# Squared products taken out of PSUM by one ScalarE operation, fp32 masked scores in the second batch, another bank for the last outputs

## The chip, the core and the metric

The program runs on one core of a Trainium2 chip. TensorE multiplies, VectorE and ScalarE do element-wise work, GpSimd clears small tiles, and SyncE issues the transfers. The engines run side by side, each taking its own instructions in order and waiting on semaphores for the others. The metric is the time of one execution in microseconds (us), as the median of several.

## The reference

Three layers follow one another for each of four batches of 768 rows and 384 columns (8 heads of 48):

```python
# 1. a recurrence over the rows t, per batch and head, with a 48x48 complex state
S_re, S_im = ar * S_re - ai * S_im + k[t] v[t]^T, ar * S_im + ai * S_re
y[t] = q[t] @ S_re
# 2. mixing of rows, then of channels
u  = x + (relu(x^T @ w_tok1) @ w_tok2)^T
z  = u + relu(u @ w_ch1) @ w_ch2
# 3. a gated layer on z mixed with the row before it
xk, xr = mu_k * z + (1 - mu_k) * z_prev, mu_r * z + (1 - mu_r) * z_prev
out = sigmoid(xr @ w_r) * (relu(xk @ w_k) ** 2 @ w_v)
```

## The kernel before

**The attention** turns the recurrence into products. The rows of a batch are cut into six blocks of 128 (J = 0 to 5). Sums of the logarithms of the decays (tiles X1, X2, X3) give factors for q and k. For each block, VectorE and ScalarE make q and k in two fp16 parts, a high and a low one (`qh`, `ql`, `kh`, `kl`); the DMA engines transpose them into the tile Rc; TensorE makes the scores `sp` of four heads at a time (stage `s_f`, groups g = 0 and 1); VectorE masks them into `m` (`s_m`, L656); and TensorE multiplies them with v into the output bank `y` (`s_h`, L668), to which the product of q with the carried state is added. `s_u` and `s_v` carry the state on, in the bank `u`. `s_i` (L689) takes `y` out of PSUM as `xh` and `xl`.

In batch 0 the masked scores meet v in fp32: one product a head. In batches 1 to 3 they are split into two fp16 parts in Rc: a ScalarE copy in `s_m` and a VectorE subtraction in `s_g` (L662). Then three fp16 products a head are made, high with high, high with low and low with high, with v split in the same way (`vh`, `vl`, `s_w`). The bank of `sp`, the bank of `y` and the place of the split scores exist once in these batches.

**The dense layers** run after the attention of their batch, beside the attention of the next one. In `two_layers` (L803) a first product makes a hidden tile of 128 columns and 384 rows in one of two PSUM banks (`ps`); it is taken out of PSUM as two fp16 parts (`part`, shown as `g`); and two tiles later the second product uses these. For w_k the way out is `wk1_out` (L907): ScalarE rectifies `ps` in place, squares it in place and copies it to the high part, then VectorE subtracts to get the low part. Only then is the bank free for the next but one hidden tile.

**What sets the order.** `ORD0` and `ORD1` list the stages of an attention step with the block each works on (`h01` is `s_h` with g = 0 on the block before). Each generator yields estimated costs, and the dense layers and the attention are interleaved by these. A scheduler places the instructions on the engines by priorities (`P_PE`, `P_EV`). So instructions near an edit can change places on every engine. The loads of the next batch's decays (`X<-by_time_a_re`) are issued behind the transposes of blocks 3 and 5. ScalarE squares them when they have landed, and VectorE adds the squares (`X3<-X3,wide`) and takes a minimum (`stat_rmin`).

Batches are counted from 0 in the code (`b`); "the second batch" below is b = 1.

Of the kernel before, what the change touches and what calls it, by code (L numbers as in the profile page):

```python
# [8 lines left out]
F32 = mybir.dt.float32  # L9
# [9 lines left out]
C = H * D  # L19
# [81 lines left out]
def split_path(  # L101
# [38 lines left out]
    tri32 = [const.tile([128, 128], F32, name=f"tri32{i}") for i in range(2)]  # L140
    ones32 = [const.tile([128, 128], F32, name=f"ones32{i}") for i in range(2)]
    last32 = const.tile([128, 128], F32, name="last32")
    anti = const.tile([128, 128], F16, name="anti")
# [56 lines left out]
    def setup_small():  # L200
        nc.sync.dma_start(out=col_c, in_=c_col)
        t = tmps.tile([128, 512], F32, tag="tmp", name="tri32")
        nc.sync.dma_start(out=t[:, 0:384], in_=c_tri)
        nc.gpsimd.tensor_copy(tri, t[:, 0:128])
        nc.gpsimd.tensor_copy(anti, t[:, 128:256])
        for i, sc in enumerate((2.0 ** L_S, 2.0 ** F_S / (2.0 * math.pi))):
            ACT(tri32[i], t[:, 0:128], ACTF.Copy, scale=sc)
            nc.gpsimd.memset(ones32[i], sc)
        ACT(last32, t[:, 256:384], ACTF.Copy)
        for t in qk16.values():  # L210
            nc.gpsimd.memset(t, 0.0)
# [116 lines left out]
    def attention(b):  # L328
# [201 lines left out]
        def load(J, names):  # L530
            if J < NJ:
                d = st.setdefault(J, {})
                ts = slice(128 * J, 128 * J + 128)
                if "q" in names:
                    t = two.tile([128, 2, C], F32, tag="hl", name="qk") if b == 0 else CH[:, 0:2]
                    d["q"], d["k"] = hd(t[:, 0]), hd(t[:, 1])
                    queue(nc.sync.dma_start(out=t, in_=qk[b, ts]))
                if "v" in names:
                    t = CH[:, J % 2 if b == 0 else 2]
                    d["v"] = hd(t)  # L540
                    queue(nc.sync.dma_start(out=t, in_=v[b, ts]))
# [24 lines left out]
        def s_b(J):  # L566
            d = st[J]
            d["vh"], d["vl"] = hd(v16[:, J % 2]), hd(v16[:, 2 + J % 2])
            d["q2"], d["k2"] = (W[:, i].rearrange("p h c d -> p c h d") for i in range(2))
            if b > 0 or J == 0:  # L570
                turn(J)
            for nm, X, i in (("q", X3, 0), ("k", X1, 1)):
                w = hd(X[:, J])
                STT(w, d[nm], col_c[:, i:i + 1], w, op0=MUL, op1=MUL)
            if b > 0:
                load(J + 1, "q")
            return 1.33

        def s_w(J):
# [3 lines left out]
            if J == 0:  # L583
                seen(d["vh"][:, :, 0:LOW_N // H])
            if b > 0:
                load(J + 1, "v")
# [67 lines left out]

        def s_m(J, g):
            m = st[J]["m", g] = tmps.tile([128, 512], F32, tag="tmp", name="m").rearrange("p (i t) -> p i t", i=4)  # L656
            TT(m, st[J]["S", g], tri.unsqueeze(1).to_broadcast([128, 4, 128]), op=MUL)
            if b > 0:
                ACT(M16[g][0], m, ACTF.Copy)
            return 0.6  # L660

        def s_g(J, g):  # L662
            if b == 0:
                return 0.0
# [3 lines left out]
        def s_h(J, g):  # L668
            d = st[J]
            if g == 0:  # L670
                d["y"] = bank("y", J, [128, H, D])
            y = d["y"]
            with tc.high_priority(offset=P_PE):
                for h in range(4 * g, 4 * g + 4):
                    if J > 0:
                        th, tl = hd(T16[0:96, J % 2]), hd(T16[0:96, 2 + J % 2])
                        for n_, (a_, b_) in enumerate((("h", th), ("h", tl), ("l", th))):
                            MM(out=y[:, h], lhsT=Tr[J % 2]["q" + a_][0:96, h], rhs=b_[:, h], start=n_ == 0, stop=False)
                    if b == 0:
                        MM(out=y[:, h], lhsT=d["m", g][:, h % 4], rhs=d["v32"][:, h], start=J == 0, stop=True)  # L680
                    for n_, (m_, v_) in enumerate(((0, "vh"), (0, "vl"), (1, "vh")) if b > 0 else ()):
                        MM(out=y[:, h], lhsT=M16[g][m_][:, h % 4], rhs=d[v_][:, h], start=J == 0 and n_ == 0, stop=n_ == 2)
            return 0.0

        def s_i(J):
            d = st.pop(J)
            if J == 0:
                x_hl[b] = [one.tile([128, NJ, C], F16, tag=f"x{s}", name=f"x{s}") for s in "hl"]
# [21 lines left out]
        fns.update({nm + str(g): late(fn, g) for nm, fn in (("f", s_f), ("g", s_g), ("h", s_h), ("m", s_m)) for g in range(2)})  # L710
        order = [(x[0], fns[x[:-1]], int(x[-1])) for x in (ORD0 if b == 0 else ORD1).split()]

# [16 lines left out]
        load(0, "qv")  # L729
        if b == 0:  # L730
            load(1, "qv")
        if b == 0:
# [18 lines left out]
    def dense(b):  # L751
# [44 lines left out]
        def two_layers(nf, first, second, evac1, evac2, at=None):  # L796
# [3 lines left out]
            for n_ in range(len(items) + LAG):  # L800
                if n_ < len(items):
# [4 lines left out]
                    with tc.high_priority(offset=P_EV):  # L806
                        evac1(ps, part)
                        if n_ == 0:
# [25 lines left out]

        def ch1_out(ps, part):
            ACT(part[:, 0], ps, ACTF.Relu)  # L836
# [69 lines left out]

        def wk1_out(ps, part):  # L907
            ACT(ps, ps, ACTF.Relu)  # L908
            ACT(ps, ps, ACTF.Square, scale=2.0 ** (SQ_S // 2 - XK_S - WK_S))
            ACT(part[:, 0], ps, ACTF.Copy)  # L910
            last_ev[:] = [TT(part[:, 1], ps, part[:, 0], op=SUB)]  # L911

# [333 lines left out]
```

## Time and profile before

| | |
|---|---|
| time, median of 3 runs | 816.45 us (816.13 to 817.19) |
| profiled execution: its own time, and the span of its trace | 818.82 us, 817.0 us |
| TensorE busy | 741.3 us (91%) |
| VectorE busy | 581.8 us (71%) |
| ScalarE busy | 522.6 us (64%) |
| mean granted TensorE clock, of full speed | 0.974 |

Busy times count the engines' instructions; the ends of matrix products are modelled, and they overlap, so a busy TensorE may still be slower than its best. Up to about 125 us the first batch's attention runs almost alone; from there to about 320 us run the first batch's dense layers with the second batch's attention, and so on; the last batch's dense layers run alone. In the rows L337 and L482 are helpers through which the attention's instructions pass, so these are told apart by their tiles.

### The profile page before, as it was taken

How to read it: one execution, taken by the hardware profiler on the slowest of the kernel's cores; microseconds unless marked ns; L12 is line 12 of the kernel's file. 1: busy time of each engine (PE TensorE's matmuls, PEld its weight loads, DVE VectorE, ACT ScalarE, POOL GpSimd, SP SyncE). 2: the span in 40 equal slices, each digit the busy share in tenths (PEclk: the TensorE clock that was granted, in tenths of full speed). 3: DMA queues.
4: the chain of work that ended last, by engine and by line, in shares of the span. 5: the costliest groups of instructions: out<-in, count | busy, mean ns of one | idle time of the engine just before them, and what ended most of it. 6: DMA issues, size and time to landing. Idle time of an engine off the chain costs nothing.

```text
span 817.0 us, 15178 instructions
## 1 busy us (share of the span) xinstructions
PE 741.3 (91%) x6107; PEld 471.4 (58%) x6107; DVE 581.8 (71%) x1016; ACT 522.6 (64%) x988; POOL 21.3 (3%) x53
## 2 busy tenths in 40 slices
PE   0968878999989889999998989999999999999996
PEld 0557845455555455555665656566666666666553
DVE  3998978999998738887768448777776454484822
ACT  7884559777588779674568778566576532142752
POOL 3000000001010000000000000000000000010000
PEclk9987989999999999999999989999999999999998
DMA  8249983444673851052336331141333342868200
GB/s 273 78 118 205 195 264 136 130 154 118 176 137 82 194 120 49 20 122 55 62 63 120 91 85 49 46 104 26 63 62 63 81 134 79 268 198 261 103 30 33
DMA packets 137949, 94.92 MB, mean 116 GB/s; under 512 B 104592, under 2 KB 120208, under 8 KB 137872
## 3 DMA queue, kind: packets, MB, share of 16 engines
q1 hardware_dynamic: 137872, 93.88, 45.2%
q8 instruction: 50, 0.82, 0.4%
q14 instruction: 27, 0.22, 0.1%
HBM read 63.97 MB, written 4.72 MB: 84 GB/s over the span
## 4 chain that ended last, share of the span: by engine, by line
PE 47%; DVE 21%; ACT 15%; DMA 12%; issue 3%; SPq 1%; DVEq 0%; ACTq 0%
PE ps L741 22%; PE a L741 14%; PE y L482 4%; DVE X L337 4%; ACT X L337 3%; DMA X<-by_time_a_re_dram 3%; PE u L482 3%; DMA wst<-in_moe_w_k_dram 2%; DVE Wc L337 2%; PE sp L482 2%; ACT tmp L875 2%; DMA Rc<-qh 1%; DVE g L837 1%; DMA wst<-in_moe_w_v_dram 1%; DVE ql L337 1%
## 5 line engine op out<-in xcount | busy, mean ns | idle before, releaser
L741 PEld LDWEIGHTS <-wc 128*128 128x128 f16 x1728 | 166.7, 98 | 116.9 <-issue 9.5
L741 PE MATMUL ps<-uh,wc 128*128 128x384 f16 x576 | 156.3, 326 | 2.1 <-DVE ul L793 1.2
L741 PE MATMUL a<-g,wc 128*128 128x384 f16 x864 | 157.9, 326 | 0.0
L741 PE MATMUL ps<-xkh,wk 128*128 128x384 f16 x384 | 106.4, 331 | 3.5 <-DVE g L911 3.3
L741 PE MATMUL a<-wv,g 128*128 128x384 f16 x576 | 106.9, 328 | 2.5 <-ACT g L910 2.5
L836 ACT ACTIVATE g<-ps 128x384 f16<-128x384 f32 x96 | 46.4, 484 | 78.0 <-PE ps L741 76.6
L741 PE MATMUL ps<-ul,wc 128*128 128x384 f16 x288 | 93.8, 326 | 0.0
L482 PEld LDWEIGHTS <-Rc 96*128 96x128 f16 (+1 forms) x1416 | 69.8, 100 | 34.4 <-issue 13.9
L837 DVE SCALAR_TENSOR_TENSOR g<-ps,g 128x384 f16<-128x384 f32 x96 | 52.9, 554 | 37.4 <-ACT g L836 37.2
L741 PEld LDWEIGHTS <-wk 128*128 128x128 f16 x576 | 55.6, 99 | 39.9 <-issue 6.4
L741 PEld LDWEIGHTS <-g 128*128 128x128 f16 x576 | 54.9, 98 | 37.4 <-ACT g L910 3.0
L741 PE MATMUL ps<-xkl,wk 128*128 128x384 f16 x192 | 63.5, 331 | 0.0
L911 DVE TENSOR_TENSOR g<-ps,g 128x384 f16<-128x384 f32 x64 | 35.3, 553 | 35.1 <-ACT g L910 34.9
L482 PE MATMUL y<-CH,Rc 96*128 96x48 f16 (+1 forms) x912 | 42.9, 186 | 9.7 <-DVE xl L337 5.2
L908 ACT ACTIVATE ps<-ps 128x384 f32<-128x384 f32 x64 | 30.4, 476 | 30.9 <-PE ps L741 29.5
L337 DVE TENSOR_TENSOR m<-sp,tri 128x512 f32<-128x512 f32 x48 | 32.6, 685 | 20.5 <-PE sp L482 19.7
L482 PE MATMUL sp<-Rc 96*128 96x128 f16 x504 | 39.2, 225 | 8.6 <-DVE m L337 3.3
L337 DVE TENSOR_TENSOR Wc<-cs,X 128x768 f32<-128x768 f32 x48 | 44.8, 951 | 0.2
L337 ACT ACTIVATE X<-X 128x1152 f32<-128x1152 f32 x32 | 37.1, 1159 | 11.5 <-DMA X<-by_time_a_re_dram 9.6
L337 ACT ACTIVATE X<-X,col_c 128x1152 f32<-128x1152 f32 x32 | 40.0, 1252 | 1.2 <-DVE X L337 0.4
L482 PE MATMUL u<-CH,kh 128*128 128x48 f16 x320 | 36.2, 188 | 3.4 <-ACT kh L337 3.4
L337 DVE TENSOR_TENSOR Rc<-m,Rc 128x512 f16<-128x512 f32 x36 | 24.8, 689 | 18.6 <-ACT Rc L337 18.6
(212 smaller groups left out, 1377.9 us busy)
## 6 DMA issues: line engine op xcount, KB each, us to landing
wst<-in_moe_w_ch_dram SPq DMA_DIRECT2D x24, 768.0 KB, 4.4
CH<-in_qk_dram SPq DMA_DIRECT2D x18, 384.0 KB, 3.2
wst<-in_moe_w_tok_dram SPq DMA_DIRECT2D x8, 768.0 KB, 5.0
wst<-in_moe_w_k_dram SPq DMA_DIRECT2D x8, 768.0 KB, 4.5
wst<-in_moe_w_v_dram SPq DMA_DIRECT2D x8, 768.0 KB, 4.6
X<-by_time_a_re_dram SPq DMA_DIRECT2D x8, 576.0 KB, 4.8
X<-by_time_a_im_dram SPq DMA_DIRECT2D x8, 576.0 KB, 6.9
CH<-by_time_v_dram SPq DMA_DIRECT2D x24, 192.0 KB, 2.7
```

Source lines behind the costliest of these rows:

```text
L337: ins = fn(*a, **k)
L482: last_mm[:] = [nc.tensor.matmul(**k)]
L741: ins = [nc.tensor.matmul(out=ps, lhsT=lh[a_], rhs=rh[b_], start=start and n_ == 0, stop=stop and n_ == 2) for n_, (a_, b_) in enumerate(( ...
L836: ACT(part[:, 0], ps, ACTF.Relu)
L837: last_ev[:] = [STT(part[:, 1], ps, 0.0, part[:, 0], op0=MAX, op1=SUB)]
L875: ACT(w[:, 0:N], z[:, 0:N], ACTF.Copy, scale=o[:, c:c + 1])
L908: ACT(ps, ps, ACTF.Relu)
L911: last_ev[:] = [TT(part[:, 1], ps, part[:, 0], op=SUB)]
```

## The change

In `wk1_out` the bank is now left by one operation: ScalarE rectifies and scales `ps` into an fp32 tile `r` in SBUF (two of them, in the space of `h1`). In batch 0 ScalarE squares `r` in place and copies it to the high part, and VectorE subtracts from SBUF. In batches 1 to 3 ScalarE squares `r` into the high part, and VectorE squares `r` itself and then subtracts: two ScalarE operations in place of three, two VectorE operations in place of one.

The last block's outputs (J = 5, batches 1 to 3) go to the bank `u`, which the state doesn't need by then, instead of `y`.

In the second batch, `s_m` multiplies the scores by a mask `tri_v` that holds v's row factors, straight into Rc, and one fp32 product a head with the unscaled v follows; the ScalarE copy and the subtraction go. v is loaded two blocks ahead into two buffers, and `vh` and `vl` have one buffer. The stages of that batch have an order of their own.

```diff
--- before.py
+++ after.py
@@ -139,6 +139,7 @@
     tri = const.tile([128, 128], F16, name="tri")
     tri32 = [const.tile([128, 128], F32, name=f"tri32{i}") for i in range(2)]
     ones32 = [const.tile([128, 128], F32, name=f"ones32{i}") for i in range(2)]
+    tri_v = const.tile([128, 128], F32, name="tri_v")
     last32 = const.tile([128, 128], F32, name="last32")
     anti = const.tile([128, 128], F16, name="anti")
     col_c = const.tile([128, 12], F32, name="col_c")
@@ -207,6 +208,7 @@
             ACT(tri32[i], t[:, 0:128], ACTF.Copy, scale=sc)
             nc.gpsimd.memset(ones32[i], sc)
         ACT(last32, t[:, 256:384], ACTF.Copy)
+        ACT(tri_v, t[:, 0:128], ACTF.Copy, scale=col_c[:, 2:3])
         for t in qk16.values():
             nc.gpsimd.memset(t, 0.0)
 
@@ -536,7 +538,7 @@
                     d["q"], d["k"] = hd(t[:, 0]), hd(t[:, 1])
                     queue(nc.sync.dma_start(out=t, in_=qk[b, ts]))
                 if "v" in names:
-                    t = CH[:, J % 2 if b == 0 else 2]
+                    t = CH[:, J % 2 if b == 0 else 2 + 2 * (J % 2) if b == 1 else 2]
                     d["v"] = hd(t)
                     queue(nc.sync.dma_start(out=t, in_=v[b, ts]))
 
@@ -565,7 +567,7 @@
 
         def s_b(J):
             d = st[J]
-            d["vh"], d["vl"] = hd(v16[:, J % 2]), hd(v16[:, 2 + J % 2])
+            d["vh"], d["vl"] = (hd(v16[:, i]) for i in ((0, 1) if b == 1 else (J % 2, 2 + J % 2)))
             d["q2"], d["k2"] = (W[:, i].rearrange("p h c d -> p c h d") for i in range(2))
             if b > 0 or J == 0:
                 turn(J)
@@ -582,7 +584,7 @@
             STT(d["vl"], d["v"], col_c[:, 2:3], d["vh"], op0=MUL, op1=SUB)
             if J == 0:
                 seen(d["vh"][:, :, 0:LOW_N // H])
-            if b > 0:
+            if b > 1:
                 load(J + 1, "v")
             return 0.5
 
@@ -653,6 +655,10 @@
             return 0.47
 
         def s_m(J, g):
+            if b == 1:
+                m = st[J]["m", g] = R[:, 3072:3584].rearrange("p (i t) -> p i t", i=4)
+                TT(m, st[J]["S", g], tri_v.unsqueeze(1).to_broadcast([128, 4, 128]), op=MUL)
+                return 1.2
             m = st[J]["m", g] = tmps.tile([128, 512], F32, tag="tmp", name="m").rearrange("p (i t) -> p i t", i=4)
             TT(m, st[J]["S", g], tri.unsqueeze(1).to_broadcast([128, 4, 128]), op=MUL)
             if b > 0:
@@ -660,7 +666,7 @@
             return 0.6
 
         def s_g(J, g):
-            if b == 0:
+            if b <= 1:
                 return 0.0
             TT(M16[g][1], st[J]["m", g], M16[g][0], op=SUB)
             return 0.6
@@ -668,7 +674,7 @@
         def s_h(J, g):
             d = st[J]
             if g == 0:
-                d["y"] = bank("y", J, [128, H, D])
+                d["y"] = bank("u" if b > 0 and J == NJ - 1 else "y", J, [128, H, D])
             y = d["y"]
             with tc.high_priority(offset=P_PE):
                 for h in range(4 * g, 4 * g + 4):
@@ -676,14 +682,16 @@
                         th, tl = hd(T16[0:96, J % 2]), hd(T16[0:96, 2 + J % 2])
                         for n_, (a_, b_) in enumerate((("h", th), ("h", tl), ("l", th))):
                             MM(out=y[:, h], lhsT=Tr[J % 2]["q" + a_][0:96, h], rhs=b_[:, h], start=n_ == 0, stop=False)
-                    if b == 0:
-                        MM(out=y[:, h], lhsT=d["m", g][:, h % 4], rhs=d["v32"][:, h], start=J == 0, stop=True)
-                    for n_, (m_, v_) in enumerate(((0, "vh"), (0, "vl"), (1, "vh")) if b > 0 else ()):
+                    if b <= 1:
+                        MM(out=y[:, h], lhsT=d["m", g][:, h % 4], rhs=d["v32" if b == 0 else "v"][:, h], start=J == 0, stop=True)
+                    for n_, (m_, v_) in enumerate(((0, "vh"), (0, "vl"), (1, "vh")) if b > 1 else ()):
                         MM(out=y[:, h], lhsT=M16[g][m_][:, h % 4], rhs=d[v_][:, h], start=J == 0 and n_ == 0, stop=n_ == 2)
             return 0.0
 
         def s_i(J):
             d = st.pop(J)
+            if b == 1:
+                load(J + 2, "v")
             if J == 0:
                 x_hl[b] = [one.tile([128, NJ, C], F16, tag=f"x{s}", name=f"x{s}") for s in "hl"]
             xh, xl = x_hl[b]
@@ -708,7 +716,8 @@
         cq, ck = late(s_c, "q"), late(s_c, "k")
         fns = {"a": s_a, "x": s_x, "l": s_l, "b": s_b, "w": s_w, "q": cq, "k": ck, "e": s_e, "i": s_i, "u": s_u, "v": s_v}
         fns.update({nm + str(g): late(fn, g) for nm, fn in (("f", s_f), ("g", s_g), ("h", s_h), ("m", s_m)) for g in range(2)})
-        order = [(x[0], fns[x[:-1]], int(x[-1])) for x in (ORD0 if b == 0 else ORD1).split()]
+        ORDB = "b0 u1 w0 v1 q0 f01 m01 f11 k0 h01 m11 e0 h11 i1"
+        order = [(x[0], fns[x[:-1]], int(x[-1])) for x in (ORD0, ORDB, ORD1, ORD1)[b].split()]
 
         def step(s):
             at[0] = s
@@ -727,8 +736,8 @@
                 ins = nc.sync.dma_start(out=X[:, half(k)], in_=src[b, 384 * k:384 * k + 384].rearrange("(j p) c -> p j c", p=128))
                 behind([ins], issued.get((b - 1, NJ - 1 if b == 1 else min(3 * k + 3, NJ - 1)), ()))
         load(0, "qv")
-        if b == 0:
-            load(1, "qv")
+        if b <= 1:
+            load(1, "qv" if b == 0 else "v")
         if b == 0:
             h1_ps.extend((ps_a.tile([128, C], F32, tag="a2", name="h1a"), ps_1.tile([128, 512], F32, tag="s", name="h1b")))
             nc.tensor.matmul(out=h1_ps[1], lhsT=tri, rhs=qk16["qh"][:, 0:4], start=True, stop=True)
@@ -804,7 +813,7 @@
                     first(t, f, ps)
                     part = gring.tile([128, 2, N], F16, tag="g", name="g")
                     with tc.high_priority(offset=P_EV):
-                        evac1(ps, part)
+                        evac1(ps, part, f)
                         if n_ == 0:
                             seen(part[:, 0, 0:LOW_N])
                     parts[t, f] = part
@@ -832,7 +841,7 @@
             for c in range(3):
                 mm3(ps, [w[:, c, 128 * f:128 * f + 128] for w in wc1], [x[:, c] for x in u[t]], c == 0, c == 2)
 
-        def ch1_out(ps, part):
+        def ch1_out(ps, part, f):
             ACT(part[:, 0], ps, ACTF.Relu)
             last_ev[:] = [STT(part[:, 1], ps, 0.0, part[:, 0], op0=MAX, op1=SUB)]
 
@@ -904,11 +913,16 @@
             for c in range(3):
                 mm3(ps, [w[:, c, 128 * f:128 * f + 128] for w in wk], [x[:, c] for x in xk[t]], c == 0, c == 2)
 
-        def wk1_out(ps, part):
-            ACT(ps, ps, ACTF.Relu)
-            ACT(ps, ps, ACTF.Square, scale=2.0 ** (SQ_S // 2 - XK_S - WK_S))
-            ACT(part[:, 0], ps, ACTF.Copy)
-            last_ev[:] = [TT(part[:, 1], ps, part[:, 0], op=SUB)]
+        def wk1_out(ps, part, f):
+            r = one.tile([128, C], F32, tag=f"h1{'hl'[f % 2]}", name="r")
+            ACT(r, ps, ACTF.Relu, scale=2.0 ** (SQ_S // 2 - XK_S - WK_S))
+            if b == 0:
+                ACT(r, r, ACTF.Square)
+                ACT(part[:, 0], r, ACTF.Copy)
+            else:
+                ACT(part[:, 0], r, ACTF.Square)
+                TT(r, r, r, op=MUL)
+            last_ev[:] = [TT(part[:, 1], r, part[:, 0], op=SUB)]
 
         def wv2(t, f, jj, part, ps, start, stop):
             need(("v", f))
```


VectorE around block 3 of the second batch's attention, before: `m` is the masked score of one group, `Rc<-m,Rc` its low part, `X3<-X3,wide` and `stat_rmin` belong to the third batch's decays, `g` to hidden tiles of w_k.

```order
L337 TENSOR_TENSOR m_3033<-sp_3020,tri_84 128x512
...
L911 TENSOR_TENSOR g_3015<-ps_3005,g_3015 128x384
...
L337 TENSOR_TENSOR Rc_1313<-m_3033,Rc_1313 128x512
L337 TENSOR_TENSOR m_3110<-sp_3055,tri_84 128x512
L337 TENSOR_TENSOR ql_113<-Wc_1314,qh_112 128x2x8x48
L337 TENSOR_TENSOR X3_119<-X3_119,wide_3538 128x1152
L911 TENSOR_TENSOR g_3080<-ps_3070,g_3080 128x384
...
L384 TENSOR_REDUCE stat_rmin_128<-X1_117 128x1
```

The same place now; `Rc<-sp,tri_v` is the masked score.

```order
L339 TENSOR_TENSOR X3_120<-X3_120,wide_3424 128x1152
L925 TENSOR_TENSOR g_2901<-r_2902,g_2901 128x384
L386 TENSOR_REDUCE stat_rmin_129<-X1_118 128x1
L339 TENSOR_TENSOR Rc_1315<-sp_2965,tri_v_89 128x512
L934 SCALAR_TENSOR_TENSOR tmp_2982,stat_osum_126<-a0_2614,rl_2306 128x384
L934 SCALAR_TENSOR_TENSOR tmp_2988,stat_osum_126<-a1_2615,rl_2306 128x384
L934 SCALAR_TENSOR_TENSOR tmp_2994,stat_osum_126<-a2_2616,rl_2306 128x384
L925 TENSOR_TENSOR g_2959<-r_2960,g_2959 128x384
L339 TENSOR_TENSOR Rc_1315<-sp_2997,tri_v_89 128x512
```

Both masked scores of block 3 stood ahead of the third batch's squares and its minimum; now both stand behind them.

ScalarE at the same point one batch later, before: the three operations of hidden tile 5029, and the fourth batch's decays being squared in `X3<-X1` and `wide<-X2`.

```order
L337 ACTIVATE X3_119<-X1_117 128x1152
L908 ACTIVATE ps_5029<-ps_5029 128x384
L337 ACTIVATE wide_5699<-X2_118 128x1152
L909 ACTIVATE ps_5029<-ps_5029 128x384
L337 ACTIVATE qh_112<-Wc_3531 128x2x8x48
L910 ACTIVATE g_5039<-ps_5029 128x384
L908 ACTIVATE ps_5063<-ps_5063 128x384
L337 ACT_TABLE_LOAD
```

The same place now; the hidden tile here is 4920 and its first operation L918.

```order
L918 ACTIVATE r_4931<-ps_4920 128x384
L339 ACTIVATE X3_120<-X1_118 128x1152
L923 ACTIVATE g_4930<-r_4931 128x384
L339 ACTIVATE wide_5601<-X2_119 128x1152
L918 ACTIVATE r_4966<-ps_4955 128x384
L339 ACTIVATE qh_113<-Wc_3417 128x2x8x48
L923 ACTIVATE g_4965<-r_4966 128x384
```

The operation that leaves the bank now comes first, ahead of both squares of decays; before, the bank of 5029 was still held by operations behind them.

## Rows read from the trace of the kernel before

**Rows 1.** Busy time by stage, second batch's attention beside first batch's dense layers.
```profile
core 0: us, PE busy (x) PEld busy (x) DVE busy (x) ACT busy (x) POOL busy (x), PEclk, DMA share, GB/s
235.00:280.00 45.00, 38.01 (x418) 24.51 (x419) 38.61 (x74) 35.75 (x76) 0.30 (x1) 1.00 0.70 148
280.00:325.00 45.00, 40.34 (x368) 25.82 (x367) 28.26 (x45) 37.65 (x57) 0.00 (x0) 0.93 0.36 87
```

**Rows 2.** TensorE's waits, 205 to 325 us: total, times, longest.
```profile
PE y L482 <- DVE Rc L337: 3.6, 3, 2.3
PE y L482 <- DVE xl L337: 2.4, 1, 2.4
PE sp L482 <- DVE m L337: 2.2, 2, 1.3
PE u L482 <- DVE CH L337: 1.9, 2, 1.4
...
PE ps L741 <- DVE g L911: 0.5, 2, 0.3
```

**Rows 3.** TensorE's waits after 325 us, same columns.
```profile
PE ps L741 <- DVE g L911: 2.8, 2, 2.6
PE y L482 <- DVE xl L337: 2.8, 1, 2.8
```

**Rows 4.** ScalarE's groups: operation, shapes, count, busy us, mean ns, idle before.
```profile
L908 ACT ACTIVATE ps<-ps 128x384 f32<-128x384 f32 x64 | 30.4, 476 | 30.9 <-PE ps L741 29.5 <-DVE g L911 1.4
...
L337 ACT ACTIVATE Rc<-m 128x512 f16<-128x512 f32 x36 | 22.4, 623 | 12.1 <-DVE m L337 5.9 <-PE y L482 5.8
...
L877 ACT ACTIVATE xkh<-tmp 128x384 f16<-128x384 f32 x24 | 12.4, 516 | 2.5 <-DVE tmp L876 2.5
L893 ACT ACTIVATE rl<-ps 128x384 f32<-128x384 f32 x24 | 11.7, 489 | 19.2 <-PE ps L741 18.0 <-PE u L482 1.1
```

**Rows 5.** VectorE's groups, same columns.
```profile
L911 DVE TENSOR_TENSOR g<-ps,g 128x384 f16<-128x384 f32 x64 | 35.3, 553 | 35.1 <-ACT g L910 34.9
...
L337 DVE TENSOR_TENSOR Rc<-m,Rc 128x512 f16<-128x512 f32 x36 | 24.8, 689 | 18.6 <-ACT Rc L337 18.6
...
L878 DVE SCALAR_TENSOR_TENSOR xkl<-tmp,xkh 128x384 f16<-128x384 f32 x24 | 13.2, 550 | 0.8 <-ACT xkh L877 0.7
```

**Rows 6.** TensorE in order of time, fp32 products of the first batch: start, length.
```profile
78.35 0.24 PE L482 MATMUL y<-CH,Rc 96*128 96x48 f16 x3
78.43 0.40 PE L482 MATMUL y<-v32l,m 128*128 128x48 f32 x2
78.67 0.24 PE L482 MATMUL y<-CH,Rc 96*128 96x48 f16 x3
```

**Rows 7.** TensorE, fp16 products of four heads, second batch, and what follows.
```profile
286.26 0.76 PE L482 MATMUL y<-CH,Rc 96*128 96x48 f16 x24
286.87 0.81 PE L741 MATMUL a<-wv,g 128*128 128x384 f16 x4
```

**Rows 8.** VectorE, the third batch's squares and minimum.
```profile
280.83 1.35 DVE L337 TENSOR_TENSOR X<-X,wide 128x1152 f32<-128x1152 f32 x1
...
284.03 1.35 DVE L384 TENSOR_REDUCE stat_rmin<-X 128x1 f32<-128x1152 f32 x1
```

**Rows 9.** ScalarE, the third batch's first loads of decays arrive.
```profile
272.73 1.17 ACT L337 ACTIVATE X<-X 128x1152 f32<-128x1152 f32 x1 [2.33 <-DMA X<-by_time_a_re_dram]
...
274.23 1.16 ACT L337 ACTIVATE wide<-X 128x1152 f32<-128x1152 f32 x1
```

**Rows 10.** TensorE, scores of block 3, second batch, first four heads.
```profile
269.72 0.83 PE L482 MATMUL sp<-Rc 96*128 96x128 f16 x12
```

**Rows 11.** ScalarE, one hidden tile of w_k, second batch: first operation.
```profile
442.31 0.47 ACT L908 ACTIVATE ps<-ps 128x384 f32<-128x384 f32 x1
```

**Rows 12.** VectorE, the last operation on the same hidden tile.
```profile
447.35 0.56 DVE L911 TENSOR_TENSOR g<-ps,g 128x384 f16<-128x384 f32 x1 [0.37 <-ACT g L910]
```

**Rows 13.** VectorE, masked scores' low part of block 5, third batch.
```profile
485.06 0.68 DVE L337 TENSOR_TENSOR Rc<-m,Rc 128x512 f16<-128x512 f32 x1
```


## The prediction

> **What bounds the kernel now.** I read the engines' shares first, then busy time by stage, then TensorE's waits, then the time order around the longest of them. TensorE is busy 741 of 817 us, so little can be won that isn't a wait of TensorE, or a slow clock after one. The stage the change touches most is 205 to 325 us, where the second batch's attention runs beside the first batch's dense layers. In 235 to 280 us the columns read: TensorE 38.0 of 45, VectorE 38.6, ScalarE 35.8; nobody has room. In 280 to 325 ScalarE has 37.7 of 45, and TensorE's clock averages 0.93 of full speed [rows 1]. The waits of TensorE there are short and many: for low parts of masked scores 3.6 us, for the bank of the outputs 2.4, for the mask 2.2, for the carried state 1.9, for a hidden tile's bank 0.5 [rows 2]. After 325 us only a few waits concern the change: 2.8 us for hidden tiles' banks and 2.8 for the output bank [rows 3].
>
> **The change, part by part.** The profiled execution took 818.8 us (span 817.0), 2.4 above the median of the runs; I work out a difference and set it against either.
>
> *fp32 products, +6.0.* In the first batch a head with a state takes 0.32 us from start to start: three fp16 products and one fp32 one, which shows as two records [rows 6]. In the second batch 24 fp16 products take 0.61 us until the next work starts, 0.025 each [rows 7]. So the fp32 product takes 0.32 - 3 x 0.025 = 0.24 us, and the three that it replaces 0.076. With 8 heads and 6 blocks that is 48 x 0.165 = 7.9 us more TensorE time. Some of it falls into waits that stay; the bounds are 2 and 7.9, and I take three quarters, since the heads of a group follow one another directly.
>
> A page speaks to this price: the Trainium skill, "FP8 and Floating Point Precision", section "TensorE Precision Notes", has true fp32 as four passes through the array. By four passes of 0.025 us the product would cost 0.10 us and the term would be 1.2 us, not 7.9; the two records and their spacing [rows 6] don't agree, and they decide.
>
> *The split of the scores goes, -4 to -6.* Each of 12 groups loses a ScalarE copy (0.62 us) and a VectorE subtraction (0.69 us) [rows 4, 5], 7.5 and 8.3 us of two full engines. The waits for the low parts, 3.6 us, and some 0.5 for the high part go with them: -4.1. The relief should also bring the masks and the state forward; of 4.1 us of such waits [rows 2] I take 2. Loading v two blocks ahead hides its loads as before; the single `vh` has to wait for the state's products, but ScalarE takes the state out directly behind, so that wait is there anyway: 0.
>
> *A new queue in front of block 3's masks, +3.5.* This I take from the order, and its time from the rows. Both masks of block 3 now stand on VectorE behind the third batch's squares and minimum, which wait for loads. Here the load let ScalarE start at 272.73 and the second squares end at 275.4 [rows 9]. Then come VectorE's sum (1.35), a subtraction (0.55) and the minimum (1.35) [rows 5, 8], and the mask itself, about 0.69 like the subtraction it resembles: some 279.2. The first group's scores began at 269.72 and were done at 270.6 [rows 10]. One bank holds them, so the second group has to wait for the mask, with only nine dense products between, some 1.6 us (four took 0.81 [rows 7]). That is up to 279.2 - 270.6 - 1.6 = 7.0 us. But TensorE comes there later by up to 24 heads of 0.165, 4 us, while the load hangs on the transposes. Bounds 0 and 7; I take the middle.
>
> *The last outputs in bank `u`, -2.6.* In the second batch the wait of 2.4 us goes, since the fp32 products need nothing but the mask. In the third batch the 2.8 us don't go: the low part of the scores there starts at 485.06 on VectorE [rows 13], and the wait ends with `xl`, just ahead of it there; products with the low part would stop for it in turn. I take 0.2 of it. The fourth batch shows no such wait.
>
> *The bank left after one operation, -3.3.* The hidden tile at 442 us kept its bank from 442.3 to 447.9 us [rows 11, 12], because squares of decays lay between ScalarE's operations and a load between these; TensorE stood 2.6 us for it [rows 3]. Leaving takes some 0.48 us now. All of 0.5 + 2.8 should go. The tile `r` has two buffers, so the same delays can stop the rectification two tiles later, which is later than before; 0.
>
> *The load on the engines in batches 1 to 3, 0.* ScalarE goes from three operations of 0.48 to two of 0.49 and 0.52 (SBUF to SBUF as in `xkh`) [rows 4], 48 times -0.43, that is -20 us; VectorE gets 48 operations of 0.55 [rows 5] more, +26 us. VectorE is at some half of the time from 440 us on and nothing there waits for it long, so I price neither. What would uncover it is a low part arriving later than the second product wants it, two hidden tiles on. In batch 0 three operations stay, each up to 0.04 us longer: 16 x 0.1 = 1.6 us of ScalarE.
>
> ScalarE's destination is where a page speaks against the change: "ScalarE: Activation LUTs", "Step-by-step: what each stage is for", in the Trainium skill, calls PSUM the faster port for this engine. The trace agrees in the sign: 476 ns in place in PSUM, 489 to SBUF, 516 from SBUF to SBUF. By it alone the change would lose some 64 x 0.013 = 0.8 us of ScalarE time, hidden but for the first batch.
>
> *The clock, -1.5.* From 280 to 325 us 7% of the clock is missing, 3.1 us [rows 1]; stretches at 1.2 in place of 2.4 GHz follow the waits of 2.3 and 2.4 us. The second wait goes, the first is replaced by block 3's. Half: -1.5.
>
> Sum: +6.0 - 4.1 - 2.0 + 3.5 - 2.6 - 3.3 - 1.5 = **-4.0 us**, so 814.8 for this execution and **812.4** for the median.
>
> **Rivals.**
>
> *The waits fall away and nothing replaces them: 803.* TensorE reaches block 3 late enough that the queue costs 0, the fp32 products fall half into waits (+4), the carried state and the masks come in time (-4), the clock stays up (-3.1): 4 - 4.1 - 4 - 2.6 - 3.3 - 3.1 = -13.1. For it speak the two full engines that lose 16 us together; against it that loads of decays stop ScalarE and VectorE as before.
>
> *Slower, by the fp32 products and the queue: 824.* One mechanism: TensorE becomes the bound of this stage, and stands once for block 3's mask. All 7.9 us show, the queue costs 7.0, and its wait brings 1.7 us of slow clock; against this -4.1 for the low parts, -2.4 for the bank, -2.6 for the hidden tile: +7.5. It decides from the point where queue and products together pass 10 us. For it speaks that TensorE has 7 us free of 45 at most [rows 1] and the products' price is measured; against it that more than half of the price is given back by waits that certainly go.
>
> *No change that can be measured.* The stage is paced by VectorE's other work, and each wait that goes is found again at the next stage letter, with the banks' 3.3 us against the queue's 3.5: about 816.
>
> *Four passes, as the page on precision has it:* 6.7 us less than the full price, 807 to 808. The rows show two records and 0.24 us, so 2 in 100.
>
> **Chances.** Forecast 0.44 (its own range 806 to 815), all waits away 0.15, four passes 0.02, no change 0.13, slower 0.26. A measurement of this kernel can tell about 0.2%, 1.6 us, from no change. Faster: 0.44 + 0.15 + 0.02 less 0.01 of the forecast's edge, 0.60; same 0.13 and that 0.01, 0.14; slower 0.26. The range of 8 in 10 is 801 to 823: it leaves out the far ends of the first two rivals.
>
> **What would show it.** The fp32 products: 0.32 us a head in the second batch's outputs. The split: no wait of `y` for Rc there, and VectorE some 8 us less busy between 205 and 325. The queue: a wait of `sp` for the mask, behind the minimum, of 3 us or more. The banks: no wait of `ps` for the subtraction of `wk1_out` over 0.5 us, and no wait of `y` for `xl` in the second batch; one of about 2.5 us in the third batch, for Rc. The forecast is wrong if the first batch's dense layers end over 3 us later than before, or if the later batches change by more than 5 us, which would mean that VectorE's added squares, or ScalarE's relief, count after all.

## The result and the profile after

The changed kernel takes 808.88 us (median of 7 runs, 805.56 to 813.28), the kernel before 817.52 us beside it. The ratio is 0.990 (95% interval 0.987 to 0.992), so 8.3 us less (6.3 to 10.5). A second measurement beside later experiments gave 0.991 (0.987 to 0.994). The forecast, 812.4, had the sign and about half of the size.

The page of the profiled execution, span and three engines (busy us, share, instructions):

```profile
span 807.1 us, 15061 instructions
PE 743.6 (92%) x6059; PEld 478.4 (59%) x6059; DVE 597.1 (74%) x1052; ACT 499.0 (62%) x929; POOL 19.8 (2%) x53
```

VectorE has 15 us more work than before, ScalarE 24 us less, TensorE 2 us more, and still the span is 10 us shorter. So waits of TensorE went, and in this execution some slow clock too: its mean over the span is 0.980 in place of 0.974, about 5 us. The stage of [rows 1], by the same view:

```profile
235.00:280.00 45.00, 41.82 (x415) 28.70 (x414) 38.69 (x72) 37.68 (x76) 0.00 (x0) 1.00 0.63 144
280.00:325.00 45.00, 42.49 (x364) 29.00 (x363) 24.83 (x41) 34.66 (x57) 0.00 (x0) 1.00 0.30 78
```

TensorE is now busy 84 of 90 us there, and its clock stays at full speed. (The same kernel again, e12, shows 0.96 in the second of these stretches.) Its waits from 205 to 325 us, which answer to [rows 2]:

```profile
PE u L484 <- DVE CH L339: 3.6, 3, 2.6
PE ps L750 <- DVE g L846: 1.5, 1, 1.5
PE sp L484 <- DVE Rc L339: 1.4, 2, 1.1
PE u L484 <- DVE Rc L339: 1.3, 1, 1.3
```

No wait is left for a low part of the scores (3.6 us before), for `xl` (2.4) or for a hidden tile's bank (0.5). The wait for the carried state (CH) has doubled. After 500 us one line of the kernel before matters that I hadn't counted, and one answers to it after the change. Before, the second product of w_k waited for ScalarE's third operation:

```profile
PE a L741 <- ACT g L910: 2.5, 2, 1.3
```

After, the same product waits for VectorE's subtraction:

```profile
PE a L750 <- DVE g L925: 0.5, 2, 0.4
```

Between 400 and 500 us the two long waits of [rows 3] are replaced by these:

```profile
PE u L484 <- ACT Rc L339: 1.7, 1, 1.7
PE u L484 <- DVE Rc L339: 1.2, 1, 1.2
PE sp L484 <- DVE m L339: 0.8, 1, 0.8
```

The hidden tiles' operations, as groups (count, busy us, mean ns, idle before):

```profile
L918 ACT ACTIVATE r<-ps 128x384 f32<-128x384 f32 x64 | 30.9, 483 | 43.0 <-PE ps L750 42.9
L923 ACT ACTIVATE g<-r 128x384 f16<-128x384 f32 x48 | 24.9, 519 | 1.1
...
L921 ACT ACTIVATE g<-r 128x384 f16<-128x384 f32 x16 | 8.3, 521 | 0.2
```

They are within 0.01 us of the lengths that [rows 4] led me to (0.49, 0.52 us).

**Where the time went, by stage.** The table gives the change of a stage's length against the kernel before, in us. A stage runs between the starts of the same numbered dense products (128x384, fp16; 3484 in each trace), so it compares equal dense work; the end is the last of them. The times in the head are those before. Ahead of 147.7 us there is nothing to explain: nearly all instructions are the same there, yet single executions of these kernels differ by up to 4.7 us. They differ later on as well: the changed kernel, its second measurement, e5 and e6 carry out the same instructions in the same order on TensorE, VectorE and ScalarE up to some 415 us, and their first stage reads -1.7, -2.2, -4.1 and +0.2. So a single entry of 4 us or less says little, and what counts is what repeats from trace to trace. How large a difference is, the ratios tell.

| us, from 147.7 | to 281.0 | to 324.1 | to 437.0 | to 494.4 | to the end | sum |
|---|---|---|---|---|---|---|
| changed | -1.7 | -1.4 | -1.2 | -4.0 | -1.0 | -9.3 |
| changed, again (e12) | -2.2 | -0.2 | -1.2 | -4.2 | -0.6 | -8.3 |
| `wk1_out` alone (e1) | -1.3 | +0.6 | -0.1 | -4.9 | -1.6 | -7.4 |
| bank `u` alone (e2) | -0.4 | +1.0 | +0.5 | -0.2 | +3.0 | +3.8 |
| fp32 scores alone (e3) | -0.3 | 0.0 | +0.4 | -1.0 | +1.9 | +1.0 |
| `wk1_out` and `u` (e4) | -2.4 | -0.4 | +0.3 | -5.0 | -0.3 | -7.9 |
| three ScalarE operations (e5) | -4.1 | -1.4 | -1.2 | -0.6 | +0.9 | -6.6 |
| bank held (e6) | +0.2 | +0.2 | -3.4 | +1.4 | +1.0 | -0.6 |
| fp32 products twice (e7) | +1.1 | +0.8 | +2.2 | -3.0 | -1.9 | -0.8 |
| fp32 in some blocks (e8) | -6.2 | +3.1 | -1.2 | -5.7 | -0.8 | -10.7 |
| last blocks in fp32 (e9) | -2.1 | -1.9 | -2.9 | +5.2 | +4.5 | +2.7 |
| masks in the ring (e10) | -3.1 | -1.9 | -1.2 | -3.2 | -1.3 | -10.6 |
| `wk1_out` in all batches, `u` (e11) | -4.9 | -0.8 | 0.0 | -5.0 | -1.5 | -12.2 |

The largest gain that repeats stands in 437 to 494 us, the end of the third batch's attention, and it comes with `wk1_out` alone: -3.0 to -5.7 in the eight traces that have that part whole, -1.0 to 0 in those without it. TensorE's own time shows what it consists of. Idle is a stage's length less TensorE's busy time in it; the clock's share is the part of the length by which its mean clock falls short of full speed (us; e9 is left out, since a wait of its own lies there).

| | idle, 437 to 494 | idle, 494 to the end | slow clock, 437 to 494 |
|---|---|---|---|
| before; e2; e3 | 5.5; 6.3; 6.8 | 4.9; 7.2; 6.4 | 3.4; 1.7; 0 |
| half of `wk1_out`'s change: e5; e6 | 5.1; 6.3 | 5.6; 5.5 | 3.4; 1.8 |
| all of it: changed, e1, e4, e7, e8, e10, e11, e12 | 1.9 to 3.8 | 3.1 to 4.3 | 0 to 3.3 |

The idle time goes with the change: over both stages 12.4 us in the mean of the first row's traces, 6.6 in that of the last row's. The slow clock doesn't: it is 0 in e3 without the change and 3.3 in e7 with it.

### The profile page after: what moved, and what is told of

Read it like the earlier page. It is cut to its first block, busy times and chain, and to the rows that moved or that the text cites. A ratio compares the mean times of both kernels' runs of the same rounds, so it can differ in the third digit from the quotient of the medians.

```text
span 807.1 us, 15061 instructions
## 1 busy us (share of the span) xinstructions
PE 743.6 (92%) x6059; PEld 478.4 (59%) x6059; DVE 597.1 (74%) x1052; ACT 499.0 (62%) x929; POOL 19.8 (2%) x53
## 4 chain that ended last, share of the span: by engine, by line
PE 51%; DVE 22%; ACT 11%; DMA 11%; issue 3%; SPq 1%; DVEq 0%; ACTq 0%
PE ps L750 23%; PE a L750 16%; PE y L484 4%; PE u L484 3%; DVE X L339 3%; ACT X L339 2%; DMA wst<-in_moe_w_k_dram 2%; DVE Wc L339 2%; PE sp L484 2%; DVE tmp L885 2%; DMA X<-by_time_a_re_dram 2%; DMA CH<-by_time_v_dram 2%; DVE ql L339 1%; DMA Rc<-kl 1%; ACT tmp L884 1%
## 5 line engine op out<-in xcount | busy, mean ns | idle before, releaser
L750 PE MATMUL a<-wv,g 128*128 128x384 f16 x576 | 105.2, 326 | 0.5 <-DVE g L925 0.5
L918 ACT ACTIVATE r<-ps 128x384 f32<-128x384 f32 x64 | 30.9, 483 | 43.0 <-PE ps L750 42.9
L924 DVE TENSOR_TENSOR r<-r 128x384 f32<-128x384 f32 x48 | 26.6, 554 | 24.4 <-ACT g L923 24.3
L339 ACT ACTIVATE X<-X 128x1152 f32<-128x1152 f32 x32 | 37.1, 1161 | 10.2 <-DMA X<-by_time_a_re_dram 8.1
L484 PE MATMUL y<-CH,Rc 128*128 128x48 f16 (+2 forms) x728 | 41.6, 195 | 0.4 <-DVE Rc L339 0.2
L750 PE MATMUL ps<-wr,xrh 128*128 128x384 f16 x144 | 35.7, 325 | 2.8 <-DVE g L846 2.7
L925 DVE TENSOR_TENSOR g<-r,g 128x384 f16<-128x384 f32 x64 | 35.5, 554 | 3.4 <-ACT g L921 1.7
```

The lines of the kernel that those rows point to most:

```text
L339: ins = fn(*a, **k)
L484: last_mm[:] = [nc.tensor.matmul(**k)]
L750: ins = [nc.tensor.matmul(out=ps, lhsT=lh[a_], rhs=rh[b_], start=start and n_ == 0, stop=stop and n_ == 2) for n_, (a_, b_) in enumerate(( ...
L918: ACT(r, ps, ACTF.Relu, scale=2.0 ** (SQ_S // 2 - XK_S - WK_S))
L924: TT(r, r, r, op=MUL)
L925: last_ev[:] = [TT(part[:, 1], r, part[:, 0], op=SUB)]
```

## The experiments

**e1, the squared products' way out alone.**

```diff
-            ACT(ps, ps, ACTF.Relu)
-            ACT(ps, ps, ACTF.Square, scale=...)
-            ACT(part[:, 0], ps, ACTF.Copy)
+            ACT(r, ps, ACTF.Relu, scale=...)      # then as in the change; scores and bank of y as before
```

> The kernel before with the squared products' way out of PSUM alone changed. Theory of the prediction: only the banks' waits count, 0.5 + 2.8 us, so -3.3 us. Second theory, from the trace after: the three operations of ScalarE also held the first products of wv2 (two waits, 2.5 us before and 0.5 after), so -5.3 us. Rival: VectorE's 48 added squares and multiplications (+26 us) slow other work, so 0 or above.

809.77 us, ratio 0.990 (0.985 to 0.994): -8.5 us, all of the change's gain and more than any of the three theories gave; the interval, -5.1 to -11.9, leaves the second, -5.3, just possible. Its waits from 400 to 500 us:

```profile
PE y L482 <- DVE xl L337: 2.6, 1, 2.6
PE sp L482 <- DVE m L337: 0.8, 1, 0.8
PE a L741 <- DVE g L916: 0.4, 1, 0.4
```

The wait for the hidden tile's bank is gone. The wait for `xl` is still there, but the slow clock that came with it is not. From 435 to 495 us, the kernel before:

```profile
435.00:495.00 60.00, 54.51 (x541) 35.98 (x539) 33.33 (x54) 46.12 (x75) 0.00 (x0) 0.94 0.46 101
```

and e1:

```profile
435.00:495.00 60.00, 56.73 (x569) 36.78 (x567) 44.22 (x77) 47.57 (x73) 0.00 (x0) 1.00 0.48 111
```

The mean clock, the third number from the end, goes from 0.94 to 1.00: 6.8 us of these 60 ran at 1.2 in place of 2.4 GHz before, which costs 3.4 us. In this execution 2.6 us of a bank and up to 3.4 of the clock fell away together. That the clock's part is the change's doing isn't shown: the mean granted clock over the whole span is 0.974 in the six runs of e1 and 0.973 in the 23 of the kernel before beside them, and 0.976 for both kernels in e12, under 1 us either time. Only e4 has more, 0.977, some 3 us.

**e2, the last outputs in bank `u` alone.**

```diff
-                d["y"] = bank("y", J, [128, H, D])
+                d["y"] = bank("u" if b > 0 and J == NJ - 1 else "y", J, [128, H, D])
```

> The kernel before with the last block's outputs in bank u alone. Theory: each of the waits for xl (2.4 us in the second batch, 2.8 in the third) becomes a wait for the low part of the masked scores, so the gain is small, -1 to -2.6 us, slow clock included. Rival: both waits go with their slow clock, -6 us or more.

818.12 us, ratio 1.001 (0.998 to 1.003): nothing, less than even the first theory. Its waits from 205 to 325 us:

```profile
PE y L482 <- DVE Rc L337: 3.3, 3, 2.3
PE u L482 <- ACT Rc L337: 2.5, 1, 2.5
```

The 2.4 us for `xl` became 2.5 us for the high part of the same scores, on the next product. What had been late was ScalarE and VectorE, not the bank.

**e3, the fp32 scores alone** (the change without its other two parts).

```diff
-            ACT(M16[g][0], m, ACTF.Copy)          # second batch
-            TT(M16[g][1], st[J]["m", g], M16[g][0], op=SUB)
+                TT(m, st[J]["S", g], tri_v..., op=MUL)   # and one fp32 product a head, own order, two v
```

> The kernel before with the second batch's fp32 masked scores alone (two buffers of v and its own order too). Theory of the prediction: +6.0 - 4.1 - 2.0 + 3.5 and some of the slow clock, so +1.5 to +3.5 us. Rival: the queue in front of the last masks costs 1.5 rather than 3.5 and the waits that go pay for the products, -2 to 0 us. Second rival: TensorE is the bound there, +7 us.

817.36 us, ratio 1.000 (0.997 to 1.003). The products' price and the waits that go cancel out. The first rival is the nearest: no wait for a mask over 0.8 us, so no queue of 3.5; by time alone, 2 us either way, the theory's +1.5 isn't excluded. Its longest waits from 205 to 325 us are now the state and `xl`:

```profile
PE u L484 <- DVE CH L339: 3.8, 3, 2.6
PE y L484 <- DVE xl L339: 1.9, 1, 1.9
```

In the third batch it has the kernel before's waits, 3.4 us for banks and 2.8 for `xl`, and yet a clock of 1.00:

```profile
435.00:495.00 60.00, 53.21 (x530) 34.56 (x528) 33.90 (x56) 47.34 (x77) 0.00 (x0) 1.00 0.45 101
```

**e4, both edits of the banks, no fp32 scores** (e1's and e2's diffs together).

> Both edits of the banks without the fp32 scores. If the parts add up, the sum of the two single runs; theory: -6 us. If the fp32 scores are what pays in the second batch, this is 2 us or more slower than the whole change (809); if they cost net, it is faster than the whole change.

810.98 us, ratio 0.990 (0.987 to 0.994): as e1, and as the whole change. The three ratios can't be told apart, so bank `u` and the fp32 scores together add 0 +- 4 us.

**e5, early bank, but ScalarE's old load.**

```diff
-            if b == 0:
+            if b >= 0:
                 ACT(r, r, ACTF.Square)
                 ACT(part[:, 0], r, ACTF.Copy)
```

> The changed kernel, in which every batch leaves PSUM by the Relu and then does Square, copy and subtraction (three operations of ScalarE, one of VectorE, as the first batch). The bank comes free as early; ScalarE's relief of 48 x 0.43 us and VectorE's 48 squares are gone. If the early bank is what pays: within 2 us of the changed kernel (809). If ScalarE's relief pays: 813 or more.

812.31 us, ratio 0.992 (0.989 to 0.995), between both expectations. The stage from 437 to 494 us loses nearly all of its gain. ScalarE there, behind a load of decays and up to the last block's scores:

```profile
470.43 1.16 ACT L339 ACTIVATE X<-X 128x1152 f32<-128x1152 f32 x1
471.50 0.47 ACT L918 ACTIVATE r<-ps 128x384 f32<-128x384 f32 x1
471.87 1.15 ACT L339 ACTIVATE wide<-X 128x1152 f32<-128x1152 f32 x1
472.92 0.51 ACT L920 ACTIVATE r<-r 128x384 f32<-128x384 f32 x1
473.33 0.57 ACT L339 ACTIVATE xh<-y,col_c 128x384 f16<-128x384 f32 x1
473.80 0.52 ACT L921 ACTIVATE g<-r 128x384 f16<-128x384 f32 x1
474.21 0.62 ACT L339 ACTIVATE Rc<-m 128x512 f16<-128x512 f32 x1
```

One more operation (`r<-r`, 0.5 us) stands in front of the scores' high part, and TensorE's wait for that part was

```profile
PE u L484 <- ACT Rc L339: 2.4, 1, 2.4
```

in place of 1.7 (1.8 in e12), with a mean clock of 0.94 from 435 to 495 us (0.97 in the changed kernel). Of the 3.4 us that the stage is longer here, 2.1 are idle time and the rest is the clock. A single wait doesn't carry the reading, since e10, with the changed kernel's code for that batch, shows 2.6 us for the same part; what e5 has more is idle time over the whole stage. Nor is the clock shown to hang on that half microsecond. e7 has ScalarE's relief and waits no longer than 1.5 us from 400 to 500 us, and its clock is 0.94 as well:

```profile
435.00:495.00 60.00, 57.21 (x565) 37.15 (x564) 42.96 (x77) 45.48 (x67) 0.00 (x0) 0.94 0.46 106
```

**e6, ScalarE relieved, but the bank held** until VectorE has multiplied:

```diff
-                TT(r, r, r, op=MUL)
+                STT(r, ps, 0.0, r, op0=MAX, op1=MUL)      # behind the Square, which reads r
```

> The changed kernel, in which VectorE's multiplication of batches 1 to 3 takes one of its factors from PSUM, behind ScalarE's Square, so that the bank is held through Relu, Square and multiplication; two operations of ScalarE and two of VectorE as changed. If the early bank pays: the waits for banks come back and it takes 813 to 816. If the engines' load pays: 809, within 2 us of the changed kernel.

812.72 us, ratio 0.994 (0.991 to 0.996), again between. The waits for the bank come back, 400 to 500 us:

```profile
PE ps L750 <- DVE r L925: 2.4, 2, 1.7
```

So e5 and e6 each give back part of the gain: 2 and 3 us by their ratios, though both intervals overlap with that of the change. In their traces TensorE stands idle from 437 us on for 10.7 and 11.8 us, near the kernel before (10.4) and not the changed one (6.9; 7.2 in e12). So in these traces either part alone pays little there, and they pay together; one execution of each is too little to split the gain between them.

**e7, each fp32 product of the second batch twice.**

```diff
-                        MM(out=y[:, h], lhsT=d["m", g]..., start=J == 0, stop=True)
+                        for n_ in range(1 + b):
+                            MM(out=y[:, h], lhsT=d["m", g]..., start=J == 0 and n_ == 0, stop=n_ == b)
```

> The changed kernel with each of the second batch's 48 fp32 products done twice (their sum goes into the outputs, which so hold the local part twice). If TensorE sets the pace of that stage: 48 x 0.23 = 11 us more, 820. If the products fall into waits for VectorE and ScalarE as the prediction has for a quarter of them: +8 us, 817. Rival, the stage is paced by VectorE: under +4 us.

815.98 us, ratio 0.998 (0.995 to 1.001) against 0.990: +6.8 us, or 0.14 us for each of 48 added products of 0.23. So some 60% shows on the path and the rest falls into waits; the middle theory is the nearest. The difference is known to 3.3 us either way, so to between a third and nine tenths.

**e8, fp32 only in blocks 3 to 5 of the second batch and the last of the third.** In this run blocks 0 to 2 multiply with parts of v that the next block may have written already; the work is the same in kind and number.

```diff
+        def late32(J):
+            return J in {1: (3, 4, 5), 2: (5,)}.get(b, ())
```

> The changed kernel with fp32 masked scores where low parts were waited for alone: blocks 3 to 5 of the second batch and the last of the third; the other blocks split their scores as before. The products cost 32 x 0.15 = 4.8 us in place of 7.2, and the third batch's waits for the parts of its last scores (1.7 + 1.2 us and 3.4 us at half clock) go. If the waits of blocks 0 to 2 stay away: -4 us, 805. Rival: VectorE's subtractions come back in front of the state and it is within 2 us of the changed kernel.

810.33 us, ratio 0.991 (0.987 to 0.994): the rival's time, but not its mechanism. The state is waited for only 0.8 us from 205 to 325 us; what is back are 2.0 us for the high parts of the split scores and 0.6 for `xl`. That these pay for the cheaper products is argued, not shown.

**e9, fp32 only in the last block of the second and third batch,** on e4, order and buffers as before.

```diff
+        def late32(J):
+            return b in (1, 2) and J == NJ - 1
```

> The kernel before with both edits of the banks, and fp32 masked scores in the last block of the second and third batch only, masks in the ring of work tiles; order and buffers of v as before. It keeps what paid (bank and relief of ScalarE, -8.5 us in e1) and pays 16 x 0.15 = 2.4 us of products for the waits of the last blocks' parts (1.6 + 2.6 us at 300 to 303 us and 1.7 + 1.5 us at 478 to 480 us in e4, slow clock beside). If these waits go: -2 to -4 us against e4 and the changed kernel, 806 to 808. Rival: the mask itself becomes the wait, as at 308 us in the changed kernel, and it is within 2 us of them, 809 to 811.

822.15 us, ratio 1.006 (1.003 to 1.008): slower than before, outside both expectations. The loss stands from 437 us on, and the trace shows only part of it, as the profiled execution (817.05 us) was the fastest of twelve. VectorE in the third batch:

```profile
466.50 1.35 DVE L386 TENSOR_REDUCE stat_rmin<-X 128x1 f32<-128x1152 f32 x1 [3.13 <-DMA X<-by_time_a_re_dram]
470.95 0.56 DVE L920 TENSOR_TENSOR r<-r 128x384 f32<-128x384 f32 x1 [3.11 <-ACT g L919]
471.55 0.56 DVE L921 TENSOR_TENSOR g<-r,g 128x384 f16<-128x384 f32 x1
472.02 0.61 DVE L339 SCALAR_TENSOR_TENSOR xl<-y,col_c,xh 128x384 f16<-128x384 f32 x1
472.55 0.55 DVE L920 TENSOR_TENSOR r<-r 128x384 f32<-128x384 f32 x1
473.02 0.68 DVE L339 TENSOR_TENSOR m<-sp,tri_v 128x512 f32<-128x512 f32 x1
```

Its scores were done at 468.3 us, and the mask stands behind a minimum that waits 3 us for a load, then behind squares that wait for ScalarE's own load-fed work. TensorE's waits from 400 to 500 us:

```profile
PE sp L484 <- DVE m L339: 5.4, 2, 3.3
```

and its clock averaged 0.91 from 435 to 495 us. A mask that the scheduler puts behind a load costs what the prediction feared, in another batch. The 4.5 us after 494 us are waits too (8.7 us idle, 4.3 in e4), spread over several products; what makes them I haven't traced.

**e10, the fp32 masks in the ring of work tiles.**

```diff
-                m = st[J]["m", g] = R[:, 3072:3584]...
+                m = st[J]["m", g] = tmps.tile([128, 512], F32, tag="tmp", name="m")...
```

> The changed kernel with the second batch's masked scores in the ring of work tiles in place of the one place beside the transposed q and k, so that the second group's mask no longer waits until the first group's products are done. If that dependency delays the masks (VectorE idled 3.9 us in front of two of them): -2 us, the waits for the mask (1.4 + 1.3 us) go. Rival: those waits come from VectorE's other work, no change within 1 us, or the ring is short of tiles and it is slower.

812.61 us, ratio 0.994 (0.992 to 0.997), beside 0.991 for the changed kernel: no gain. The waits for the mask stay (205 to 325 us):

```profile
PE u L484 <- DVE m L339: 1.4, 1, 1.4
PE sp L484 <- DVE m L339: 1.1, 2, 0.7
```

so the single place isn't what they come from; that VectorE's other work is, as the rival has it, remains argued.

**e11, the short way out in the first batch too,** on e4.

```diff
-            if b == 0:
+            if b < 0:
                 ACT(r, r, ACTF.Square)
                 ACT(part[:, 0], r, ACTF.Copy)
```

> Both edits of the banks (e4) with the form of batches 1 to 3 in the first batch too: two operations of ScalarE and two of VectorE. If ScalarE sets the pace beside the second batch's attention: -2 us against e4, 809. If VectorE does: +3 us or more, 814, since 16 operations of 0.55 us are 8.8 us more on it.

805.73 us, ratio 0.986 (0.982 to 0.991), the lowest median of all, without any fp32 scores. It lies 1.4% below the kernel before. Its lead over the changed kernel (0.990 and 0.991) and over e4 (0.990) is within the intervals. From 205 to 325 us:

```profile
205.00:325.00 120.00, 109.48 (x1057) 69.43 (x1056) 106.87 (x188) 92.81 (x163) 2.59 (x5) 0.99 0.55 125
```

VectorE is busy 107 of 120 us, 10 more than in e4 (96.8), and the kernel isn't slower for it, against the +3 us of the second expectation. TensorE is 3 us more busy in this stretch, and the stage up to 281 us is 2.5 us shorter than in e4. That ScalarE's queue was what came last there isn't shown: equal instructions differ by 4.3 us in that stage.

**e12, the changed kernel again:**

> The changed kernel again, on the same chip as the three runs beside it: a ratio of 0.990 to the kernel before, as measured first (0.987 to 0.992).

810.11 us, ratio 0.991 (0.987 to 0.994).

## Why the prediction was right, and where it was not

Sign and range held. The -3.3 for leaving the bank was too small by more than half; the rest of the sum, -0.7, measured 0 +- 4 us, with errors among its terms that cancelled, so that part of the number was luck. In TensorE's time it is an exchange: from 147.7 to 324 us it stood idle 15.3 us in e4 and 10.2 and 9.5 in the two traces of the changed kernel, where it was busy 5 to 6 us longer.

By one of its own signs the forecast was wrong: the later batches were to change by no more than 5 us, and from 324 us on they changed by -6.2 (-6.0 in e12, -6.6 in e1).

*The bank left after one operation, -3.3, and the load on the engines, 0: the terms that were mis-sized.* Together they measured -8.5 us (e1). The waits I named did go: 2.6 us at 448 us and 0.5 in the second batch. The interval of e1 is -5.1 to -11.9. Two things were missing. First, the second product's own wait for ScalarE's third operation: 2.5 us before, 0.5 after; it stood in the view of waits that I had open, and I passed it over because the line didn't name the bank. e2 and e3, which keep the old way out, show 3.3 and 2.9 us for it. Second, and the real mistake, I priced 20 us of relief on ScalarE at nothing; the prediction gives a reason for VectorE, which is at some half of the time, and none for ScalarE. In the third batch that engine isn't idle where it matters: its work bunches behind the loads of decays, and without the relief (e5) TensorE's idle time from 437 us on is that of the kernel before. The slow clock at 484 us, 3.4 us of the profiled execution, isn't shown to be a third thing: over all runs the clock differs by under 1 us with and without this part (e1). The idle time makes some 6 of the 8.5 us; where the rest lies stays open. Of VectorE's 26 us more nothing shows, as I had it; e11 adds 9 us on it in the fullest stage and is no slower.

*fp32 products, +6.0: right in price.* Four heads with a state:

```profile
276.56 1.43 PE L484 MATMUL y<-CH,Rc 96*128 96x48 f16 x20
277.83 0.49 PE L750 MATMUL ps<-wr,xrh 128*128 128x384 f16 x2
```

1.27 us for four, so 0.32 a head as in [rows 6], and the four passes of the rival are out. e7 shows 60% of the price on the path; I took three quarters.

*The split goes, -4.1, and the relief for masks and state, -2.0.* The first half is right. The 12 subtractions, 8.2 us of VectorE, did go between 205 and 325; it lost only 4.6 us there (94.5 to 89.9), since later work moved into these 120 us. The relief is wrong: masks 2.2 to 1.4 us, but the state 1.9 to 3.6.

*The queue in front of block 3's masks, +3.5: order right, cost 0.* VectorE after the change:

```profile
270.69 1.35 DVE L339 TENSOR_TENSOR X<-X,wide 128x1152 f32<-128x1152 f32 x1
271.96 0.55 DVE L925 TENSOR_TENSOR g<-r,g 128x384 f16<-128x384 f32 x1
272.43 1.34 DVE L386 TENSOR_REDUCE stat_rmin<-X 128x1 f32<-128x1152 f32 x1
273.69 0.68 DVE L339 TENSOR_TENSOR Rc<-sp,tri_v 128x512 f32<-128x512 f32 x1
```

The sum, subtraction, minimum and mask stand as I read them from the order. But the load came earlier, as SyncE's queue shows. Before:

```profile
266.57 0.44 SPq L727 DMA_DIRECT2D X<-by_time_a_re_dram  x1
```

and after:

```profile
259.75 0.58 SPq L736 DMA_DIRECT2D X<-by_time_a_re_dram  x1
```

6.8 us earlier, because the transposes that it stands behind came sooner and v is no longer loaded in front of it (0.5 us). I had kept the load where it was, while moving TensorE only. The first scores of block 3 came at 272.0 us, and TensorE didn't wait. TensorE's long wait there is now for the state, 2.6 us up to 268.7 us, the wait that I had going down. It ends before the sum and the minimum begin, so it isn't theirs. The state's operation stands on VectorE behind work on the next q and k that waits for their load:

```profile
264.98 1.15 DVE L339 SCALAR_TENSOR_TENSOR X<-CH,col_c,X 128x384 f32<-128x384 f32 x2 [1.85 <-DMA CH<-in_qk_dram]
267.91 0.61 DVE L339 SCALAR_TENSOR_TENSOR CH<-u,col_c,CH 96x384 f16<-96x384 f32 x1
```

e9 shows that a mask behind the minimum does cost time.

*The last outputs in bank `u`, -2.6: 0.* In the third batch it went as written, one letter further (1.7 us for the high part and 1.2 for the low). In the second it was to pay 2.4 with the fp32 scores; what is left there is a wait for the mask, 1.3 us, against 1.9 in e3, so some 0.6.

*The clock, -1.5.* From 280 to 325 us it rose from 0.93 to 1.00, all of the 3.1 us, in one execution, and to 0.96 in e12 with the same instructions; e6, again with the same instructions, is at 0.96 over 205 to 325. So the term can't be read from a single trace. Of the rivals "all waits fall away" was right that the queue costs 0, but it had the masks and the state in time and some 10 of its 13 us won up to 325 us; 2.4 to 3.1 were, and most of the gain lies after 400 us.

## What to carry to other kernels

An engine's average share says little about what an operation on it is worth: look at the bunch of work behind each load, and ask which product of TensorE waits for the last of it. Whoever takes a wait away should ask at once which operation of the same engine is late next: moving the outputs to another bank only changed the letter of the wait. When an order is changed, the loads move too; price a queue only after placing the load that feeds it anew. And before a stage of one trace is explained, see how far traces of the same instructions differ there.

## What the runs showed of the hardware that was not expected

Wait and slow clock don't go together in a fixed way. In e1 TensorE waited 2.6 us for `xl` and kept 2.4 GHz (1.00 from 435 to 495 us), and so it did in e3 with waits of 2.8 and 2.2 us; with 2.8 us in the kernel before, in e5 with 2.4 and in e7 with no wait over 1.5, the mean of that stretch was 0.94. What decides it these runs don't show. Also, the first 148 us of these kernels, almost the same instructions, took between 143 and 148 us from execution to execution; most of that spread was there by the first dense product (3.7 us less in e2, 0.6 more in e1). The waits for transposes differ by under 1 us there, but the mean clock from 50 to 80 us was 0.72 in the kernel before and 0.83 in e2.
